# A recurrent attention block feeding a multiplicative FFN: the first group of the bridge tensor is carried on chip by thirty small DMAs, and three chunks' output stores change place in SyncE's queue

## The chip, the cores and the metric

The kernel runs on one core of one Trainium2 chip. The metric is the time of one execution on the device, in microseconds; lower is better. A profiled execution also has a span, the time from its first to its last instruction.

Five engines run side by side, each through its own list of instructions in order: TensorE (PE in the profile, its weight loads PEld), VectorE (DVE), ScalarE (ACT), GpSimd (POOL) and SyncE (SP). They wait for each other by semaphores. SP computes nothing here: it issues DMAs, which the core's 16 DMA engines carry out. SBUF is the on-chip memory of 128 partitions, PSUM the memory that TensorE writes to (eight banks here), DRAM the memory off the chip.

## What is computed

Two blocks follow each other. The first is a gated linear recurrence over 768 steps, for 4 batches and 8 heads of width 48; the second is a feed-forward block over the 3072 tokens that result, with 384 features:

```python
for t in range(S):
    state = alpha[:, :, t, :, None] * state + np.einsum('bhd,bhe->bhde', k[:, :, t], v[:, :, t])
    y[:, :, t] = np.einsum('bhd,bhde->bhe', q[:, :, t], state)
...
x = y.transpose(0, 2, 1, 3).reshape(B * S, H * D)     # 3072 x 384
a = x @ w1                                            # 384 x 1024
b = x @ w2
h = a * b @ w3                                        # 1024 x 1024
out = h @ w_out                                       # 1024 x 384
```

q, k, v and alpha are float32. The four weights are float64; the kernel reads them as pairs of 32-bit words ("raw") and converts them itself.

## The kernel before

**Chunks and groups.** The 3072 tokens are cut into 24 chunks of 128 tokens, six a batch. Three chunks make a group of 384 tokens; there are eight groups. In the first part of the program, `for n in range(N + 1)`, chunk n goes through the recurrence, and as soon as the first groups are complete the first layers of the feed-forward block (the "gates") are mixed in. The second part finishes the gates, folds w3 with w_out and projects.

**One chunk.** Its k and q arrive in a tile `kq` of 128 tokens x 2 x 8 heads x 48 (`load_kq`, lines 153 and 154: two DMAs of 192 KB in runs of 192 bytes), its alpha in a tile `ac` (line 147, 192 KB; chunks 2 to 7 in pairs, line 143). ScalarE takes the logarithm of alpha, TensorE sums it along the chunk (`decays`), ScalarE exponentiates. Then:

- `decayed`, line 359, on VectorE: `qk` = k and q times the decays. Iteration n does it for chunk n + 2.
- `transposed`, line 381, on TensorE: `qk` turned, for chunk n + 1 in iteration n; ScalarE copies it out of PSUM (line 383).
- `scores`, line 454, on TensorE, for chunk n; VectorE masks the scores into `ms` (line 457).
- `attend_state` (line 474) and `attend` (line 485), on TensorE, for chunk n - 1; ScalarE copies the result out of PSUM into the tile `x` (line 489): partitions 0 to 47 hold the even half of the heads' features, partitions 64 to 111 the other, so that a head has 48 partitions. `outer` (line 393) updates the state.

**Weights.** Beside this, raw pieces of w1 and w2 of 512 KB are loaded by SP (line 236, in `to_fp32`) and converted in steps by ScalarE and VectorE (lines 244 to 265; `convert` and `fetch` deal them out, `raws` says how many pieces may be under way). A third part of the split weight is made on TensorE (`third`, lines 276 and 277) and copied by ScalarE (line 278).

**The bridge.** `attend` appends two stores of the tile `x` to the list `later`: to `xd`, a tensor in DRAM for each group, in the layout features x tokens. `store()`, the first call of each iteration, issues them on SP (line 305: 96 KB each, 192 runs of 512 bytes). When a group is complete, `load_x` reads `xd` back into the tile `xT` of 128 partitions x 3 x 384 tokens (line 501, 576 KB); for group 0 that is done in iteration 4. `split_x` makes from `xT` the three parts of `x3` that the gates multiply with (line 507 on ScalarE, 508 and 509 on VectorE); for group 0 in iteration 6 = `FIRST`. The gates' matrix products are line 515. Every group's `xd` is read back again in the second part, for the other half of the gates.

**What sets the order.** Each engine runs its list in order. The list is not the order of the source: a scheduler of the tile framework sorts the instructions of each engine by its own estimate of when their inputs come, within the marks that the program sets (`after_marks`). SP's list holds all loads of q, k, v, alpha and raw weights and the stores together, in the order of their calls. The framework gives SP's DMAs eight completion semaphores in turn: in the built program each DMA on SP first waits until the DMA eight places ahead of it, which uses the same semaphore, has landed. The trace shows the same: eight semaphores in rotation, each DMA waiting for the one that it will update. So SP has at most eight DMAs under way.

The iteration's beginning, in the source:

```python
store()
if n in loads:
    load_x(loads[n])
if n != 1 and not 2 < n <= FIRST:
    load_a(n + 5)
...
for m in (n + 3,) * (n <= FIRST) + (n + 4,) * (n >= FIRST):
    load_kq(m)
    if 2 < n <= FIRST and m == n + 3:
        load_a(n + 5)
    if n < FIRST - 2:
        fetch(raws)
```

Of the kernel before, what the change touches and what calls it, by code (L numbers as in the profile page):

```python
# [10 lines left out]
FP32 = mybir.dt.float32  # L11
# [37 lines left out]
def kernel(  # L49
# [12 lines left out]
    nc = tc.nc  # L62
    B, H, S, D = q.shape
    C = 128
# [5 lines left out]
    DP = 64  # L70
    Q = 32
    KM = DM // C
# [3 lines left out]
    TG = G * C  # L76
# [8 lines left out]
    def pool(name, bufs, stack=ctx, **kw):  # L85
        return stack.enter_context(tc.tile_pool(name=name, bufs=bufs, **kw))
# [3 lines left out]
    xp = pool("xp", 1)  # L90
# [18 lines left out]
    st, mark = {}, {}  # L109

    def after_marks(*names):
        stack = ExitStack()
        for x in names:
            stack.enter_context(tc.issue_after(mark[x]))
        return stack
# [5 lines left out]
    xd = [dram.tile([DM, TG], FP32, name=f"xd{g}") for g in range(NG)]  # L121
# [9 lines left out]
    def rows(src, n):  # L131
        b, c = divmod(n, NCH)
        return src[b, :, ds(c * C, C), :].rearrange("h p d -> p h d")

    def paired(n):
        return 2 <= n < PAIRED

    def load_a(n):
        if paired(n):
            if n % 2 == 0:  # L140
                b, c = divmod(n, NCH)
                x = pairs[n // 2 % 2]
                nc.sync.dma_start(out=x.rearrange("p h s d -> p h (s d)"), in_=alpha[b, :, ds(c * C, 2 * C), :].rearrange("h (p s) d -> p h (s d)", s=2))
                st["a", n] = st["a", n + 1] = x
        elif n < N:
            st["a", n] = inp.tile([C, H, D], FP32, tag="ac", name="ac", bufs=2)
            nc.sync.dma_start(out=st["a", n], in_=rows(alpha, n))

    def load_kq(n):
        if n >= N:  # L150
            return
        st["kq", n] = inp.tile([C, 2, H, D], FP32, tag="kq", name="kq")
        nc.sync.dma_start(out=st["kq", n][:, 0], in_=rows(k, n))
        nc.sync.dma_start(out=st["kq", n][:, 1], in_=rows(q, n))

    def load_v(n):
        if n < N:
            st["v", n] = vs[n % len(vs)]
            (nc.gpsimd if 2 < n < 8 else nc.sync).dma_start(out=st["v", n][:, :, 0:D], in_=rows(v, n))

    def turned(n):
        return TURNED <= n < N
# [117 lines left out]
    def fetch(ahead=3):  # L280
        while weights and len(begun) < ahead:
            begun.append(weights.popleft())
            next(begun[-1])
# [15 lines left out]
    later = deque()  # L299

    def store():

        while later:
            dst, src = later.popleft()
            nc.sync.dma_start(out=dst, in_=src)
# [171 lines left out]
    def attend(n):  # L477
        (y, heads), ms, vc = st.pop(("y", n)), st.pop(("ms", n)), st.pop(("v", n))
        for j, i, to in heads:
            if turned(n):  # L480
                w = vts[n % 2][:, j, :] if i else vc[:, 2 * j, :]
                nc.tensor.matmul(to[:, DP:], w, ms[:, i, j, DP:], start=False,  # L482
                                 stop=(j % HP == HP - 1), skip_group_check=True)
            else:
                nc.tensor.matmul(to, vc[:, 2 * j + i, :], ms[:, i, j, :], start=(n % NCH == 0 and j % HP == 0),  # L485
                                 stop=(j % HP == HP - 1), skip_group_check=True)
        x = work.tile([C, HP, 2, C], FP32, tag="x", name="x", bufs=4)
        for i in range(2):
            copied = nc.scalar.copy(x[:, :, i], y[i])
        ends_of_part1[1] = copied.ins  # L490
        x = x.rearrange("p j i t -> p (j i) t")

        g, c = divmod(n, G)
        to = xd[g].rearrange("(b h d) t -> b d h t", b=2, d=D)
        for half in range(2):
            later.append((to[half, :, :, ds(c * C, C)], x[ds(DP * half, D)]))


    def load_x(g, queue=nc.sync):
        st["xT", g] = xp.tile([C, KM, TG], FP32, tag="xT", name="xT")  # L500
        queue.dma_start(out=st["xT", g], in_=xd[g].rearrange("(k p) t -> p k t", p=C))

    def split_x(g, i):
        x = st.pop(("xT", g))
        t = tr[i].tile([C, 3 * KM * TG], FP32R, tag="x3", name="x3").rearrange("p (s k t) -> p s k t", s=3, k=KM)
        st["x3", g] = t
        nc.scalar.activation(t[:, 0], x, AF.Copy, scale=1.0 - 2.0 ** -13)
        nc.vector.tensor_sub(t[:, 1], x, t[:, 0].bitcast(FP32))
        mark["x3"] = nc.vector.scalar_tensor_tensor(t[:, 2], t[:, 0].bitcast(FP32), -1.0 - 1.0 / P, x,  # L509
                                                    op0=ALU.mult, op1=ALU.add).ins  # L510
# [73 lines left out]
    def gate(g, f):  # L584
        yield from (late_gate if late else early_gate)(g, f)
# [99 lines left out]
    FIRST = 6  # L685
# [1 line left out]
    loads = {8: 1, 11: 2, 15: 3, 19: 4}  # L687

    for n in range(N + 1):
        store()  # L690
        if n in loads:
            load_x(loads[n])
        if n != 1 and not 2 < n <= FIRST:
            load_a(n + 5)
        raws = (3, 3, 3, 3, 2, 2, 3, 3)[n] if n < 8 else 4
        for m in (n + 3,) * (n <= FIRST) + (n + 4,) * (n >= FIRST):
            load_kq(m)
            if 2 < n <= FIRST and m == n + 3:
                load_a(n + 5)
            if n < FIRST - 2:  # L700
                fetch(raws)
        if n >= FIRST:
            load_v(n + 2)
        if n:
            attend_state(n - 1)
        if n < N:
            scores(n)
        else:
            for j in range(NP):
                for i in range(2):  # L710
                    attend_low(n - 1, j % 2, i, i ^ (j < 2))
        transposed(n + 1)
        if n == 1:
            decays(3)
            load_a(6)
            with after_marks(("e", 3)):
                logs(4)
        if n == FIRST + 1:
            run(2)
        if n < FIRST:  # L720
            with after_marks("pool"):
                load_v(n + 2)
        if n - 2 in begin and n > FIRST:
            g, tiles = begin[n - 2]
            with after_marks(("ms", n), ("qkT", n + 1)):
                split_x(g, 0)
            fill.extend(gate(g, f) for f in tiles)
        if n == FIRST:
            with after_marks("l", ("qkT", n + 1)):
                split_x(0, 0)  # L730
            fill.extend(gate(0, f) for f in begin[n - 3][1])
        pieces = ((3, 3, 2, 0) if n > FIRST + 3 else (0, 3, 3, 0))[(n - FIRST) % 4] if n >= FIRST else 0
        if n == 0:
            with after_marks(("qkT", 0)):
                logs(2)
            decays(2)
            with after_marks(("e", 2)):
                logs(3)
        early, ready = n < FIRST, len(thirds) if n > 2 else n // 2
        marks = (*[("qkT", n + 1)] * (n < N - 1), *[("qk", n + 1), ("ms", n)] * early, *["x3"] * (n - 2 in begin and n > FIRST))  # L740
        if n < N - 2 and n != FIRST:
            with after_marks(*marks):
                convert(2 if early else 1, raws)
        advance(n)
        turn_v(n)
        if n:
            attend(n - 1)
        outer(n)
        if n > FIRST:
            third(ready)  # L750
        run(pieces > 0)
        if early:
            with after_marks(*marks):
                convert(1, raws)
        with after_marks(*[("ms", n)] * (n < 3)):
            decayed(n + 2)
        if not early:
            with after_marks(*[("qkT", n + 1)] * (n < N - 4)):
                logs(n + 4)
        if n == 4:  # L760
            load_x(0)
        convert(early and n > 0, raws)
        run(pieces > 1)
        if n:
            decays(n + 3)
        if n <= FIRST:
            third(ready)
        if 0 < n < FIRST:
            with after_marks(("e", n + 3)):
                logs(n + 4)  # L770
        if n == FIRST:
            with after_marks("x3", ("e", n + 3)):
                convert(2, raws)
        elif n < N - 2:
            convert(n == FIRST - 1 if early else n % 3 == 0, raws)
        if n == FIRST - 1:
            assert len(done) == 2 * KM
        run(pieces > 2)
        if n == N - 3:
            while begun:  # L780
                convert(1)
            weights.extend(load_out(j) for j in range(KF))
            fetch(4)
# [90 lines left out]
```

## Time and profile before

| what | value |
|---|---|
| runs | 466.03 us median of 3 (464.22 to 467.32) |
| the profiled execution's own time | 465.8 us |
| its span | 464.1 us |
| PE busy | 446.0 us (96%) |
| DVE busy | 371.1 us (80%) |
| ACT busy | 276.3 us (60%) |
| DMA packets | 148869, 80.37 MB, mean 173 GB/s |
| loads of k and of q | 24 each of 192 KB |
| stores of x to `xd` | 48 of 96 KB, 4.0 us from issue to landing (median) |
| read-back of `xd` on SP | 5 of 576 KB, 4.7 us |

The busy times are those of the whole span. The page also cuts the span into 40 slices of 11.6 us, with a digit for the busy tenths of each engine, the granted TensorE clock and the DMA engines. A "chain" view follows the program back from its last instruction, at each step to what released it. A "timeline" lists instructions with their start, their length and, in brackets, the idle time before them and what ended it. A tile's view gives the DMAs that touch it and the time from issue to landing. A busy PE is not PE at its peak, since matrix products are pipelined.

### The profile page before, as it was taken

What the parts mean: (1) busy time and instruction counts of PE and PEld (TensorE: products, weight loads), DVE (VectorE), ACT (ScalarE), POOL (GpSimd) and SP (SyncE); (2) the same over time, 40 slices, a digit from 0 to 9 for tenths busy, and PEclk for the clock granted to TensorE, in tenths of its full rate; (3) what the DMA queues carried; (4) which work ended last, traced back from release to release, by engine and by line L of the source; (5) the groups of instructions that cost most, each with busy time, mean ns of one, the idle gap of its engine ahead of it and who ended that gap; (6) DMA issues with size and microseconds to landing.
All of it is one profiled execution on the core that took longest, in us unless ns stands there. A gap on an engine that the chain in (4) does not pass through costs nothing.

```text
span 464.1 us, 11153 instructions
## 1 busy us (share of the span) xinstructions
PE 446.0 (96%) x4296; PEld 424.3 (91%) x4296; DVE 371.1 (80%) x610; ACT 276.3 (60%) x544; POOL 94.3 (20%) x186
## 2 busy tenths in 40 slices
PE   4996999899999999999999999999999999999996
PEld 2674899799999989999999999999999999999996
DVE  2886997999979989899998999997542967776671
ACT  4764984848668553989875776764544543333430
POOL 6332152215322360112221201211110000000000
PEclk9998899999999999999999999999999999999999
DMA  9999999899998965476766446412115966655511
GB/s 174 257 208 235 245 221 206 203 216 230 173 223 178 239 185 154 126 227 211 216 187 204 131 142 177 148 52 86 51 37 153 260 200 180 186 176 162 164 51 52
DMA packets 148869, 80.37 MB, mean 173 GB/s; under 512 B 97392, under 2 KB 138608, under 8 KB 148816
## 3 DMA queue, kind: packets, MB, share of 16 engines
q1 hardware_dynamic: 143040, 64.44, 57.2%
q0 software_dynamic: 5776, 15.22, 10.8%
q8 instruction: 34, 0.56, 0.6%
q14 instruction: 19, 0.16, 0.1%
HBM read 57.58 MB, written 22.06 MB: 172 GB/s over the span
## 4 chain that ended last, share of the span: by engine, by line
PE 87%; DVE 5%; DMA 4%; issue 2%; ACT 1%; SPq 0%; DVEq 0%
PE bank L515 71%; DMA kq<-in_q_dram 4%; PE bank L381 3%; PE bank L430 2%; PE bank L474 2%; PE bank L482 2%; PE bank L454 1%; PE bank L393 1%; PE bank L343 1%; PE bank L346 1%; PE bank L485 1%; PE bank L419 1%; DVE ms L457 1%; DMA ac<-in_alpha_dram 1%; DVE x L509 1%
## 5 line engine op out<-in xcount | busy, mean ns | idle before, releaser
L515 PE MATMUL bank<-x,w 128*128 128x384 f32 x1152 | 209.5, 337 | 1.0 <-DVE ms L440 0.9
L515 PEld LDWEIGHTS bank<-x,w 128*128 128x128 f32 x1152 | 200.2, 188 | 2.8 <-DVE ms L440 1.2
L515 PE MATMUL bank<-w3o,ab 128*128 128x384 f32 x576 | 100.2, 336 | 0.0
L515 PEld LDWEIGHTS bank<-w3o,ab 128*128 128x128 f32 x576 | 99.9, 188 | 0.0
L540 ACT ACTIVATE bank<-bank 128x384 f32<-128x384 f32 x96 | 45.7, 476 | 43.5 <-PE bank L515 43.2
L524 ACT ACTIVATE t<-bank 128x384 f32<-128x384 f32 x64 | 31.6, 495 | 55.1 <-PE bank L515 54.8
L590 POOL DMA_DIRECT2D abd<-ab x45 | 25.8, 573 | 137.7 <-DVE ab L576 121.5
L383 ACT COPY qkT<-bank 128x512 f32<-128x512 f32 x48 | 26.0, 593 | 24.2 <-PE bank L381 24.2
L641 DVE TENSOR_TENSOR ab<-abl,ab 128x1024 fp32r<-128x1024 f32 x24 | 29.4, 1224 | 12.5 <-ACT ab L640 12.5
L640 ACT ACTIVATE ab<-abl 128x1024 fp32r<-128x1024 f32 x24 | 25.5, 1061 | 20.2 <-PE bank L515 18.4
L515 PE MATMUL bank<-wo,w3T 128*128 128x384 f32 x192 | 35.9, 334 | 0.0
L359 DVE TENSOR_TENSOR qk<-kq,e 128x768 f32<-128x768 f32 x24 | 23.2, 966 | 15.4 <-ACT e L350 7.6
L576 DVE TENSOR_TENSOR ab<-bank,r 128x384 f32<-128x384 f32 x44 | 24.2, 550 | 12.5 <-PE bank L515 6.3
L515 PEld LDWEIGHTS bank<-wo,w3T 128*128 128x128 f32 x192 | 33.5, 188 | 0.0
L249 ACT ACTIVATE power<-power,rebias 128x512 uint32<-128x512 uint32 (+1 forms) x36 | 25.1, 698 | 11.2 <-DVE power L248 11.2
L526 DVE SCALAR_TENSOR_TENSOR o<-bank,t 128x384 f32<-128x384 f32 x24 | 13.4, 557 | 22.7 <-issue 13.7
L642 DVE SCALAR_TENSOR_TENSOR ab<-ab,abl 128x1024 fp32r<-128x1024 f32 x24 | 29.2, 1218 | 0.0
L526 DVE SCALAR_TENSOR_TENSOR r<-bank,t 128x384 f32<-128x384 f32 x40 | 22.1, 553 | 6.8 <-ACT t L524 3.4
L251 DVE SCALAR_TENSOR_TENSOR mant<-mant,rest 128x512 f32<-128x512 uint32 (+1 forms) x36 | 23.8, 661 | 3.4 <-ACT rest L244 3.3
L252 DVE SCALAR_TENSOR_TENSOR power<-raw,power 128x512 uint32<-128x512 uint32 (+1 forms) x36 | 23.6, 655 | 2.4 <-ACT power L249 2.4
L253 DVE TENSOR_TENSOR mant<-mant,power 128x512 f32<-128x512 f32 (+1 forms) x36 | 23.6, 656 | 0.5
L244 ACT ACTIVATE rest<-raw 128x512 f32<-128x512 uint32 (+1 forms) x36 | 23.3, 649 | 0.0
(102 smaller groups left out, 675.4 us busy)
## 6 DMA issues: line engine op xcount, KB each, us to landing
abl<-abd SPq DMA_DIRECT2D x24, 512.0 KB, 4.6
abd<-ab POOLq DMA_DIRECT2D x45, 192.0 KB, 3.1
raw<-in_moe_w_dram SPq DMA_DIRECT2D x64, 128.0 KB, 3.4
raw<-in_moe_w_dram SPq DMA_DIRECT2D x12, 512.0 KB, 6.2
xT<-xd POOLq DMA_DIRECT2D x9, 576.0 KB, 4.6
kq<-in_k_dram SPq DMA_DIRECT2D x24, 192.0 KB, 4.9
kq<-in_q_dram SPq DMA_DIRECT2D x24, 192.0 KB, 5.4
xd<-x SPq DMA_DIRECT2D x48, 96.0 KB, 4.0
```

Source lines behind the costliest of these rows:

```text
L249: nc.scalar.activation(power, power, AF.Relu, scale=2.0 ** 23, bias=rebias)
L251: nc.vector.scalar_tensor_tensor(mant, top, 2.0 ** -20, rest, op0=ALU.mult, op1=ALU.add)
L383: mark["qkT", n] = nc.scalar.copy(qkT[:, :, :, ds(DP * half, DP)], tp[half]).ins
L515: nc.tensor.matmul(p, w[part][i], x[part][i], start=start and part == parts[0] and i == 0, stop=stop and part == parts[-1] and i == n - 1, ...
L524: nc.scalar.activation(t, p1, AF.Copy, scale=(1.0 + 1.0 / P) * scale)
L526: nc.vector.scalar_tensor_tensor(to, p2, scale, t, op0=ALU.mult, op1=ALU.add)
L540: nc.scalar.activation(p, p, AF.Copy, scale=1.0 + 1.0 / P)
L576: nc.vector.tensor_mul(ab, p, r[0])
L590: (nc.gpsimd if late else nc.sync).dma_start(out=abd[g][:, f, :], in_=ab)
L640: nc.scalar.activation(t[:, 0], ab, AF.Copy, scale=1.0 - 2.0 ** -13)
L641: nc.vector.tensor_sub(t[:, 1], ab, t[:, 0].bitcast(FP32))
L642: nc.vector.scalar_tensor_tensor(t[:, 2], t[:, 0].bitcast(FP32), -1.0 - 1.0 / P, ab, op0=ALU.mult, op1=ALU.add)
```

## The change

The output of the first three chunks (group 0) no longer goes to `xd` and back before it is split. `attend` calls the new function `place`, which writes the tile `x` straight into the tile `xT`, from SBUF to SBUF: one DMA a head, and two where a head's 48 features lie across two blocks of 128 partitions. That makes ten DMAs a chunk, of 48, 32 or 16 partitions x 512 bytes (24, 16 or 8 KB), in place of two of 96 KB. `load_x(0)` in iteration 4 is gone. Since the second part still reads `xd[0]`, one store of the whole `xT`, 576 KB, is issued at the start of iteration 7 (`FIRST + 1`). And in iterations 2 to 5 the stores are issued after that iteration's loads of k, q and alpha and not ahead of them. `split_x` keeps `xT` in the table (no `pop`).

```diff
         g, c = divmod(n, G)
+        if g == 0:
+            return place(c, x)
         to = xd[g].rearrange("(b h d) t -> b d h t", b=2, d=D)
...
+    def place(c, x):
+
+        if ("xT", 0) not in st:
+            st["xT", 0] = xp.tile([C, KM, TG], FP32, tag="xT", name="xT")
+        for h in range(H):
+            half, j = divmod(h, H // 2)
+            f = h * D
+            while f < (h + 1) * D:
+                kk, at = divmod(f, C)
+                n = min(C - at, (h + 1) * D - f)
+                later.append((st["xT", 0][ds(at, n), kk, ds(c * C, C)], x[ds(DP * half + f - h * D, n), j]))
+                f += n
...
     def split_x(g, i):
-        x = st.pop(("xT", g))
+        x = st["xT", g]
...
     for n in range(N + 1):
-        store()
+        if not 1 < n < FIRST:
+            store()
         if n in loads:
             load_x(loads[n])
+        if n == FIRST + 1:
+            nc.sync.dma_start(out=xd[0].rearrange("(k p) t -> p k t", p=C), in_=st["xT", 0])
...
             load_kq(m)
             if 2 < n <= FIRST and m == n + 3:
                 load_a(n + 5)
+            if 1 < n < FIRST:
+                store()
             if n < FIRST - 2:
                 fetch(raws)
...
-        if n == 4:
-            load_x(0)
         convert(early and n > 0, raws)
```

**The built program.** TensorE's list is the same in both kernels. SP's has 14 rows more. The scheduler also sorts VectorE's and ScalarE's lists anew around the changed stretch:

```
VectorE, before: ms(3) w mant power qk(5) tmp .. qk(6) ms(4) w mant power T .. qk(7) ms(5) w mant power .. ms(6) w ms(6) qk(8) T x-split ..
VectorE, after:  qk(5) ms(3) w mant power tmp .. ms(4) w mant power qk(6) T .. ms(5) w mant power .. qk(7) w ms(6) T ms(7) x-split qk(8) ..
ScalarE, before: .. qkT(7) x-split x la e la e w w ..
ScalarE, after:  .. qkT(7) x e e w w x-split la ..
```

Numbers in brackets are chunks, and ".." leaves steps of a conversion out. On VectorE w, mant and power are steps of a weight's conversion; on ScalarE the "w w" are the copies of two thirds (line 278). x-split is the split of group 0 (lines 507 to 509 before, 521 to 523 after); tmp and T are updates of the state, ms(7) in the second line is its first half. Two passages carry most of the difference: qk(5) stands ahead of ms(3) and not qk(6) ahead of ms(4), and the split of group 0 stands ahead of qk(8) on VectorE and behind the copies of the thirds on ScalarE.

## The prediction

> **What bounds the kernel now.** The page first: busy shares, then the slices.
>
> ```profile
> PE 446.0 (96%) x4296; PEld 424.3 (91%) x4296; DVE 371.1 (80%) x610; ACT 276.3 (60%) x544; POOL 94.3 (20%) x186
> ...
> PE   4996999899999999999999999999999999999996
> ...
> PEclk9998899999999999999999999999999999999999
> DMA  9999999899998965476766446412115966655511
> ```
>
> From the fifth slice on (46 us), TensorE is full: the windows from 51 to 84 us and from 86 to 140 us show it busy all the time, with a gap of 1.5 us at 84. So a microsecond lost or won before the gates begin (line 515, first at 59.16 us) moves the end by as much, and the question is when TensorE gets there. The DMA engines are full just there too. The chain of the first 60 us says what TensorE waits for (start, length, what):
>
> ```profile
> 20.27 8.82 DMA kq<-in_q_dram
> ...
> 34.62 7.67 DMA kq<-in_q_dram
> 42.29 0.03 issue
> ...
> 42.84 0.25 DVE qk L359
> 43.09 0.62 issue
> 43.71 0.70 DVE ms L457
> 44.41 0.04 issue
> 44.45 0.80 PE bank L276
> ```
>
> The q of chunk 6 is issued at 34.62 and lands 7.67 us later. VectorE, which has qk(6) ahead of ms(4), is held until then, and TensorE with it: 3.59 us idle before 44.45 in its timeline. The windows show what follows (stretch, busy times of PE, PEld, DVE, ACT, POOL, then the clock, DMA share and GB/s):
>
> ```profile
> 44.00:51.00 7.00, 6.55 (x67) 5.28 (x68) 6.97 (x13) 4.21 (x9) 1.44 (x2) 0.56 1.00 228
> 51.00:59.00 8.00, 8.00 (x120) 6.36 (x122) 7.34 (x13) 7.72 (x18) 1.03 (x2) 1.00 1.09 229
> ```
>
> After the gap the clock is at half. The six groups from line 276 to line 485 take 44.45 to 50.84, 6.39 us; the same six take 51.29 to 55.26, 3.97 us, one pass later. So **a gap of that kind costs 2.4 us on top of itself**, and slows by a factor of 1.6. The change aims at this place: loads ahead of stores. SP's timeline shows what it moves (start, length, instruction):
>
> ```profile
> 28.01 1.91 SPq L305 DMA_DIRECT2D xd<-x  x2
> 30.02 0.39 SPq L153 DMA_DIRECT2D kq<-in_k_dram  x1
> ...
> 42.21 0.40 SPq L153 DMA_DIRECT2D kq<-in_k_dram  x1
> ...
> 45.94 0.37 SPq L501 DMA_DIRECT2D xT<-xd  x1
> ...
> 47.37 0.50 SPq L153 DMA_DIRECT2D kq<-in_k_dram  x1
> ```
>
> **What the moved loads gain.** k and q of chunk 5 no longer wait for a chunk's stores: those are issued at 28.01 and end at 29.92, and on the DMA engines they take from 31.71 (the raw piece ahead landing) to 32.66, 0.95 us. Chunks 6 and 7 have one chunk's stores fewer ahead of them, 0.95 us. Chunk 8 also loses the 576 KB read-back ahead of it (45.94 to 50.71; the DMA ahead landed at 48.15, so 2.56 us of service). On the engines, q(5) lands at about 35.40 - 0.95 - 0.9 (GpSimd's v, issued at 29.03, now comes behind) = 33.6. But qk(5) now stands ahead of ms(3): ms(3) begins at 33.6 + 0.1 + 0.87 = 34.5 and not at 32.26, its first half is out at 35.2, and TensorE's line 276, at 33.69 before, waits for it: 1.5 us lost. ms(4) in turn no longer waits for q(6). TensorE reached that place at 40.86; plus 1.5, less the 0.63 us it waited at 36.25, that is 41.7 and not 44.45: 2.7 us won. With the half clock gone, 2.4 more: **5.1 us ahead at 51 us**, and TensorE done with scores(6) at 53.74 - 5.1 = 48.6. This is all that the change can win.
>
> **What the small DMAs cost on SP.** A DMA on SP waits until the one eight places ahead has landed. Before, that rarely decided: six DMAs a chunk. Now a chunk has fourteen: ten pieces, raw, k, q, alpha. From 27 to 58 us the tile views give from issue to landing (shortest, median, longest) 4.0, 4.6, 5.5 for the stores of x, 4.4, 5.0, 8.0 for k and q, 4.4, 4.9, 7.5 for alpha, 6.1, 6.4, 6.8 for raw. No row has a piece of 24 KB, SBUF to SBUF; the nearest is the 96 KB store of the same tile, so I take its 4.6. Fourteen DMAs then need (10 x 4.6 + 2 x 5.0 + 4.9 + 6.4) / 8 = **8.4 us a chunk**. Before, the stores' starts 28.01, 33.17, 40.08, 46.40 and 52.88 give 6.2. The low bound is SP's own issue time: 14 x 0.43 (a store's median) = 6.0, under 6.2, no cost. The high bound has every piece at raw's 6.4: 11.2 us.
>
> At 8.4, k of chunks 5, 6, 7 and 8 is issued at 28.0, 36.4, 44.8 and 52.4 (the last without a raw piece, 0.8 less); before at 30.02, 34.13, 42.21 and 47.37. The raw piece ahead of k(7) goes out 0.9 earlier, at 43.9, and lands at 50.3; before at 38.17 and 44.56.
>
> The Trainium skill has a rule for this term: "DMA: Bandwidth & Descriptors", section "Anatomy of one DMA", gives about 2.0 us fixed plus bytes over 436 GB/s for a DMA issued by GpSimd. A piece would land after an estimated 2.06 us, before seven more are issued; SP would never wait, and the sum would be that of the low bound. [...] The stage's rows, at twice that and more, speak against it.
>
> **What that does to the engines.** VectorE now has the steps on this raw piece (lines 245 to 253) ahead of qk(7); before, qk(7) ran at 48.39 and these steps from 51.06 to 53.96, 2.9 us. So qk(7) is out at 50.3 + 0.1 + 2.9 + 0.95 = 54.2, and line 381 of chunk 7 follows at 54.25, before at 53.74. TensorE has been idle since 48.6: the 5.1 us won are lost here, 0.5 more, and the gap, longer than 3.59, brings the half clock.
>
> Then the split of group 0. Its input is no trouble: the last piece goes out just ahead of k(8), at 52, and lands at 56.6. But ScalarE now has the split behind the copies of the two thirds, and VectorE has qk(8) behind its part of the split. From line 381 of chunk 7 (53.74) to the end of the second third (57.58) TensorE took 3.84; at half clock 3.84 x 1.6 = 6.2. Then a copy 0.59, ScalarE's split 1.22, VectorE's two 1.26 + 1.35, qk(8) 0.96, and 0.3 for hops: 5.7. Line 381 of chunk 8 comes at 54.25 + 6.2 + 5.7 = 66.1; before at 58.57. **That is 7.5 us late.** TensorE ended scores(7) at about 62, so it idles 4 us again: half clock again, 2.4. (Before, line 507 ran at 55.85, under other work, and nothing of this chain was on the path.)
>
> For the clock the skill agrees with the row and adds a condition: "TensorE: Matmul & The Clock Gate", section "What's actually happening", has windows of about 3.4 us that run free, so a gap near that length may or may not halve the clock. If neither gap did, the estimate would be 4.8 us lower.
>
> **Hidden.** The store of 576 KB in iteration 7 delays what stands behind it by 2.56 us of service; TensorE, late by more than the queue, covers it, else it costs those 2.56. The 1.5 us gap at 84 stands behind the split of group 1 and stays. Later groups, GpSimd's list and the second part do the same work.
>
> **The sum.** 7.5 + 2.4 = 9.9 us late at the gates, and TensorE is full from there to the end. The profiled execution: 465.8 + 9.9 = 475.7; against the median of 466.03 about the same, and I say 475.5.
>
> **Rivals.**
>
> - *The places never bind* (pieces landing within 3.4 us, eight issues). At 6.2 us a chunk raw lands at 39.5 + 6.4 = 45.9, qk(7) is out at 49.9, line 381 of chunk 8 comes at 49.9 + 3.84 + 5.7 = 59.4, 0.9 late, with or without 2.4 for the half clock: 466.7 to 469.1. For it: the pieces touch no DRAM. Against it: they queue behind the same loads. 0.22.
> - *The places bind harder*: 11.2 us a chunk puts raw's landing at 55.9, line 381 of chunk 8 at 71.7, 13.1 late, plus 2.4: 481.3. For it: the loads' 5 to 8 us, which the pieces now stand behind. Against it: stores landed in 5.5 at most. 0.13.
> - *Faster*: the won 5.1 us stay won, 460.7. This takes q and raw of chunk 7 on time and a split off the path; it decides if TensorE's idle time ahead of line 381 of chunk 8 is nil. For it: split inputs land early. Against it: the lists as built put the split there, which gives back 5.7 + 3.84 - 4.83 = 4.7 whatever the DMAs do. 0.05.
> - *It does not do what it says*: pieces late for the split, which then waits for a landing. Over 61 us it would decide; 5 us hence. In the forecast's range or above; 0.05.
>
> The forecast itself has 0.55. A difference under 1% can't be told from none here. Slower by over 1% (from 470.7) are the forecast, the harder rival and the last one, less 0.01 that may fall short: 0.72. Same is the first rival and that 0.01: 0.23. Faster is 0.05. The range leaves out the faster end and most of the harder one: 467 to 480.5.
>
> **What would show it.** SP's DMAs near 8.4 us a chunk, with the DMA share under 1 between 34 and 56 us; qk(7) ending at 54, TensorE idle over 3.5 us ahead of line 381 of chunks 7 and 8, both with the half clock behind; line 521 beginning after 60 us. I am wrong if SP's chunk takes 6 to 7 us, if TensorE keeps its clock, or if later slack takes the delay back.

## The result, and the profile after

The changed kernel takes **480.19 us** (median of 4 runs, 479.67 to 480.80), the kernel before 465.75 (4 runs): a ratio of 1.0317, with a 95% interval of 1.0278 to 1.0355. It is slower, by 14.4 us. The prediction said 475.5, slower by 9.5, with 467 to 480.5 as its range: the sign was right, the loss was half as large again as forecast, and 480.19 lies at the very end of the range (1.0317 times the 466.03 us that the prediction started from is 480.8, just past it). The profiled execution took 479.67, with a span of 478.0; before, 465.8 and 464.1. So the spans differ by 13.9 us, and against the prediction's own sum of 9.9 there are 4.0 us to explain.

The page of the changed kernel, with the lines that answer to those shown of the kernel before:

```profile
PE 451.1 (94%) x4296; PEld 428.5 (90%) x4296; DVE 372.5 (78%) x610; ACT 278.2 (58%) x544; POOL 94.7 (20%) x186
...
PE   4989469999999999999999999999999999999996
...
PEclk9997778999999999999999999999999999999999
DMA  9997589999899996466576554532102985555511
```

PE's dip now spans the fifth and sixth slices (48 to 72 us), not the fourth alone; the clock is below full in the fourth to seventh, and the DMA engines, full there before, are at five to eight tenths in the fourth to sixth (36 to 72 us). So TensorE waits while the DMA engines have room. SP's timeline in that stretch (start, length, instruction):

```profile
37.76 0.53 SPq L236 DMA_DIRECT2D raw<-in_moe_w_dram  x1
38.39 1.26 SPq L153 DMA_DIRECT2D kq<-in_k_dram  x1
39.70 0.57 SPq L154 DMA_DIRECT2D kq<-in_q_dram  x1
40.32 2.49 SPq L147 DMA_DIRECT2D ac<-in_alpha_dram  x1
42.91 7.66 SPq L305 DMA_DIRECT2D xT<-x  x10
50.68 0.54 SPq L236 DMA_DIRECT2D raw<-in_moe_w_dram  x1
51.31 0.38 SPq L153 DMA_DIRECT2D kq<-in_k_dram  x1
```

From one raw piece to the next, 37.76 to 50.68, SP needs 12.9 us, with hardly a gap between its instructions. The prediction had 8.4. Ten pieces hold it for 7.66 us, so the raw piece ahead of k of chunk 7 goes out at 50.68, where 43.9 was forecast, and lands at 54.35. TensorE's timeline (start, length, instruction; in brackets the idle time before it and what ended it) shows the price:

```profile
58.46 1.12 PE L381 MATMUL bank<-ident,qk 64*128 64x64 f32 x16 [6.81 <-DVE qk L359]
...
64.83 1.16 PE L454 MATMUL bank<-qkT 48*128 48x128 f32 x16
70.49 0.94 PE L381 MATMUL bank<-ident,qk 64*128 64x64 f32 x16 [4.50 <-DVE qk L359]
71.36 4.69 PE L529 MATMUL bank<-x,w 128*128 128x384 f32 x18
```

These are line 381 of chunks 7 and 8, each behind a long idle time, and the first group of the gates, which at half clock takes 4.69 us (3.40 before). Line 381 of chunk 8 is 11.9 us later than before (58.57), the second group of gates 13.5 (77.46 against 63.97), the end 13.9.

### The profile page after: what moved, and what is told of

Same layout as the page of the kernel before. It is cut to its first block, busy times and chain, and to the rows that moved or that the text cites. A ratio compares the mean times of both kernels' runs of the same rounds, so it can differ in the third digit from the quotient of the medians.

```text
span 478.0 us, 11195 instructions
## 1 busy us (share of the span) xinstructions
PE 451.1 (94%) x4296; PEld 428.5 (90%) x4296; DVE 372.5 (78%) x610; ACT 278.2 (58%) x544; POOL 94.7 (20%) x186
## 3 DMA queue, kind: packets, MB, share of 16 engines
q0 software_dynamic: 5776, 15.22, 10.2%
## 4 chain that ended last, share of the span: by engine, by line
PE 83%; DMA 6%; DVE 4%; SPq 3%; ACT 2%; issue 2%; DVEq 0%; ACTq 0%
PE bank L529 70%; PE bank L430 3%; DMA kq<-in_q_dram 3%; SPq L305 3%; PE bank L381 2%; PE bank L482 2%; PE bank L474 2%; DMA ac<-in_alpha_dram 1%; PE bank L346 1%; PE bank L393 1%; DMA raw<-in_moe_w_dram 1%; PE bank L419 1%; DMA kq<-in_k_dram 1%; DMA raw<-in_moe_w_out_dram 1%; PE bank L343 1%
## 5 line engine op out<-in xcount | busy, mean ns | idle before, releaser
L381 PE MATMUL bank<-ident,qk 64*128 64x64 f32 x384 | 18.7, 241 | 14.8 <-DVE qk L359 13.8
L381 PEld LDWEIGHTS bank<-ident,qk 64*128 64x128 f32 x384 | 15.6, 150 | 18.1 <-ACT w L260 7.0
```

Of the source, the lines that this page charges most:

```text
L381: nc.tensor.transpose(tp[half][:, i, j, :], qk[s, i, 2 * j:2 * j + 2, :], ident[s, s])
```

## The experiments

The theory after reading both traces, **A**: SP is bound by the time it takes to issue a DMA, not by places or landings; thirty pieces at about 0.63 us each lengthen its chunk, and whatever stands behind them in its queue comes late. (SP issues 340 DMAs in the trace of the changed kernel and 316 in that of the kernel before: 24 more, thirty pieces and one store in place of six stores and a read-back, and not the 14 rows named above.) Rivals: **B**, the path from SBUF to SBUF or the new order costs; **C**, the prediction's places, eight at a time, wait for landings; **D**, the place of group 0's split has a price of its own. The ratios below are to the kernel before, measured on the same chip.

### Each part alone

Stores behind the loads, on the kernel before (`loads_first`):

```diff
-        store()
+        if not 1 < n < FIRST:
+            store()
...
                 load_a(n + 5)
+            if 1 < n < FIRST:
+                store()
             if n < FIRST - 2:
```

> One part of the change alone, on the kernel before: in iterations 2 to 5 the stores of x go out behind that iteration's loads; two stores of 96 KB a chunk to DRAM and the read-back of group 0 stay as they were. Theory A (the ten pieces a chunk are what costs; SP issues each in about 0.63 us): with two stores a chunk none of the 14 us appears; 461 to 467 us. Within A, if the 5.1 us that the prediction counts as won by the moved loads are real, 460.7; if the list with qk(5) ahead of ms(3) opens a pause near 34 us and so only moves the half clock there, as in the changed kernel (1.90 us idle before 35.70, clock 0.57 from 36 to 44), 464 or more. Theory B (the order of loads and stores, with the lists it brings, is what costs): 472 us or more.

Measured: 465.28 us, ratio 0.9997 (0.9982 to 1.0013). The reordering costs nothing, and it brings nothing either. The 5.1 us that the prediction counted as won are not there, though the half clock is gone. The window from 44 to 51 us (stretch; busy times of PE, PEld, DVE, ACT, POOL; clock, DMA share, GB/s):

```profile
44.00:51.00 7.00, 6.02 (x87) 4.35 (x88) 6.97 (x14) 4.97 (x11) 2.11 (x4) 1.00 1.20 211
```

At full clock TensorE now has a microsecond of small waits here, and VectorE is busy for 6.97 of 7 us. Line 454 of chunk 6 begins at 50.86 (52.74 before), 1.9 us earlier, the first gates at 58.27 (59.16), 0.9 earlier, and the span is 0.7 shorter. The pause ahead of line 276 that the expectation feared near 34 us was only 0.49 us long here, at 36 us, and the clock stayed up; so neither account of the missing gain in that expectation was right.

The ten pieces alone, with the stores ahead of the loads as before the change (`place_only`: the changed kernel with `store()` again the first call of each iteration):

> The other part alone, on the changed kernel: ten pieces a chunk on chip, but the stores go out first in every iteration, as before the change. Theory A (SP's issue time for thirty pieces): each chunk's ten pieces of 0.63 us now stand straight ahead of its k and q, SP's chunk stays at 10 to 13 us, and the time is that of the changed kernel or more: 478 to 486 us. Theory B (the loads' order costs): near the kernel before, 466 to 470.

Measured: 475.31 us, ratio 1.021 (1.0171 to 1.0248). SP's chunk is 9.5 and 10.2 us, from the starts of its ten pieces at 26.17, 35.64 and 45.86, and line 381 of chunk 7 begins at 58.59, as late as in the changed kernel. But the time is below what was expected. The last ten pieces stand ahead of k of chunk 7 in this order and not ahead of k of chunk 8, which goes out at 56.66 (61.18 in the changed kernel); line 381 of chunk 8 begins at 65.58 after 0.20 us of idle time. So of the 14.4 us some 10 come with the pieces wherever they stand, and the stores' new place, harmless by itself, adds 4 to 5 to them.

In this run, unlike in the changed kernel, the prediction's limit of eight did hold SP. Four pieces (at 30.20, 31.67, 40.38 and 41.60) go out 0.02 us after the DMA eight places ahead has landed, and the view of SP's waits from 24 to 62 us (line, what it waited for: us, times, longest) has 2.2 us of them, a little over one microsecond in each of the two chunks:

```profile
SPq L305 <- DMA raw<-in_moe_w_dram: 1.3, 2, 0.9
...
SPq L305 <- DMA xT<-x: 0.7, 1, 0.7
...
SPq L305 <- DMA x<-in_alpha_dram: 0.2, 1, 0.2
```

### The number of pieces, their size, their way

Two pieces in place of ten, same place, SBUF to SBUF (`two_pieces`):

```diff
-        for h in range(H):
...
+        for half in range(2):
+            later.append((st["xT", 0][ds(DP * half, D), :, ds(c * C, C)], x[ds(DP * half, D), 0:KM]))
```

> The changed kernel with two DMAs a chunk in place of ten, same place in SP's queue, same tiles: 48 partitions x 3 x 512 bytes each, 72 KB. The heads land in the wrong rows of the tile and one head in four is left out, so the feed-forward of group 0 computes on other data; the tile is zeroed once on GpSimd. All else does the same work. Theory A (issue time): SP is spared 8 x 0.63 = 5 us a chunk, raw ahead of k of chunk 7 goes out 7 to 10 us earlier than 50.68, and the time falls to 461 to 468 us. Theory B (what costs is the path itself, SBUF to SBUF with late landings, or the split's place): 474 us or more.

Measured: 466.62 us, ratio 1.003 (1.0009 to 1.0051). The path from tile to tile by itself is not what costs. Nor does it gain: with nearly the whole loss gone, the kernel is still no faster than with a store to DRAM and a read-back.

Ten pieces of a quarter of the length (`small_pieces`):

```diff
-  st["xT", 0][ds(at, n), kk, ds(c * C, C)],      x[ds(DP * half + f - h * D, n), j]
+  st["xT", 0][ds(at, n), kk, ds(c * C, C // 4)], x[ds(DP * half + f - h * D, n), j, 0:C // 4]
```

> The changed kernel with the ten pieces a chunk kept, but each a quarter as long (32 tokens, 128 bytes a partition, 2 to 6 KB); three quarters of group 0's input are left out and stay zero. The lists of all engines are those of the changed kernel. Theory A (SP's issue time, whatever the size): SP's chunk stays at 12 to 13 us and the time within 1.5 us of 480.2. Theory C (the prediction's: the places bind, so the landing counts, or the bytes): pieces that land sooner shorten the chunk, 475 us or less.

Measured: 480.81 us, ratio 1.0344 (1.0284 to 1.0403). A quarter of the bytes changes nothing; from one raw piece to the next SP still needs 12.1 us (37.85 to 49.98).

Five pieces a chunk (`five_pieces`: only those with `half == 0`):

> The changed kernel with only the first five of the ten pieces a chunk (the even half of the heads); the other half of group 0's input is left out and stays zero. The lists of VectorE and ScalarE come out a little different from the changed kernel's (the split of group 0 is earlier). With two pieces a chunk the time was 466.62, with ten 480.19. If each piece costs its issue time, whatever else is late (linear): 466.62 + 15 x 0.57 = 475, so 472 to 477 us. If there is a threshold (SP's chunk of four loads and five pieces, 5 x 0.63 + 2.0 to 4.9 = 5 to 8 us, is not longer than the 6.0 to 7.5 us that the engines take for a chunk, so that the pieces are hidden until SP's chunk exceeds that): 466 to 470 us.

Measured: 472.27 us, ratio 1.0148 (1.0110 to 1.0187). Two, five and ten pieces a chunk give 466.62, 472.27 and 480.19: 0.63 us for each of the first nine DMAs added and 0.53 for each of the next fifteen (0.60 and 0.49, when each is first taken against the kernel before on its own chip). That is close to the time that SP takes to issue one, 0.63 with its gap. At neither of these two steps do the added pieces hide.

Ten pieces, but to DRAM, with the read-back as before (`ten_stores`: the reordered kernel above, its two stores of the first three chunks cut at the change's borders):

```diff
+        if g == 0:
...
+                    n = min(C - f % C, (h + 1) * D - f)
+                    later.append((xd[0][ds(f, n), ds(c * C, C)], x[ds(DP * half + f - h * D, n), j]))
```

> The count without the path: x of the first three chunks goes to DRAM and is read back in iteration 4, as before the change, with the stores behind the loads, but each chunk's stores are cut into the change's ten pieces (48, 32 or 16 partitions x 512 bytes) in place of two of 96 KB; nothing is left out. Theory A (the number of DMAs on SP is what costs, wherever they go): with two stores of the same bytes this order took 465.28; with ten, SP's chunk is 10 to 13 us again and the time is 474 us or more, near 480 if a piece to DRAM takes 0.6 us to issue, near 474 if it takes the 0.43 of a 96 KB store. Rival (the way from SBUF to SBUF costs): within 2 us of 465.3.

Measured: 474.51 us, ratio 1.0202 (1.0136 to 1.0267). The same bytes on the same way take some 9 us more as ten DMAs than as two. And a piece to DRAM is issued faster than one to SBUF. The tile views of the changed kernel and of this run (length on SP, shortest, median and longest, in ns; then issue to landing):

```profile
L305 SPq DMA_DIRECT2D xT<-x x30: 536/589/2678, 29.3 to 60.1; - x30
...
DMA to landing us min/median/max: 1.7/2.5/5.5
```

```profile
L305 SPq DMA_DIRECT2D xd<-x x32: 368/420/2474, 28.9 to 61.1; - x32
...
DMA to landing us min/median/max: 1.5/2.3/5.6
```

0.59 us against 0.42 (the 32 hold two stores of chunk 3). Thirty differences of 0.17 make 5.1 us, and the two kernels lie 5.7 apart (5.3, each against the kernel before on its own chip). That the first makes the second is argued from the sizes: the two kernels also differ in the read-back.

### What stands behind the pieces

The raw weights ahead of the pieces (`raw_first`: `store()` moved behind the iteration's first `convert`, which issues them):

> The changed kernel with one swap in SP's queue: in iterations 2 and 3 the 512 KB piece of raw weights that stood behind the ten pieces of x goes out ahead of them; the lists of VectorE and ScalarE up to the gates stay. In the changed kernel SP issued ten pieces from 44.02 to 50.57, then raw at 50.68, k and q of chunk 7 at 51.31 and 51.74, which landed at 54.35, 55.40 and 56.45; line 381 of chunk 7 began at 58.46. Theory A1 (the issue time of the pieces is the loss, and q of chunk 7 is as late as raw): raw is early, but q still waits for the pieces; it lands 1 to 2 us earlier at most, line 381 of chunk 7 begins at 56 to 57.5, and the time is 477 to 479.5 us. Theory A2 (the ring raw, ScalarE's lines 244 and 249, x copy, ten pieces, next raw is the loss, and breaking it gives most of it back): 473 us or less.

Measured: 477.04 us, ratio 1.0226 (1.0172 to 1.0279), as A1 has it. The raw piece is off the path now, and qk of chunk 7 waits for q: SP issues the ten pieces from 43.27 to 50.34 and then k and q; qk begins at 54.57 (57.36 in the changed kernel), line 381 at 55.68, a little ahead of what was expected. (In the changed kernel the ten pieces begin at 42.91; 44.02 is the second one.) Whatever comes first, something that is needed is behind 7 us of pieces.

The pieces on another queue (`pool_pieces`):

```diff
-            nc.sync.dma_start(out=dst, in_=src)
+            (nc.gpsimd if len(dst.shape) == 2 else nc.sync).dma_start(out=dst, in_=src)
```

> The changed kernel with the thirty pieces issued by GpSimd in place of SP; nothing is left out. SP's chunk then has four DMAs, and its raw piece ahead of k of chunk 7 goes out before 44. Theory A (SP's issue time): the 14 us are gone unless GpSimd has no room for them: 462 to 468 us. GpSimd's DMAs took 0.5 to 0.9 us each to issue in the changed kernel, so ten pieces are 5 to 9 us a chunk there, ahead of its update of the state (line 412) that TensorE's line 474 waits for; if that decides (rival), line 474 is late in each of three chunks and the time is 470 or more.

Measured: 477.95 us, ratio 1.0251 (1.0208 to 1.0295). The rival holds: SP is free, and GpSimd is not. It needs 0.50 us a piece, and its own work stands behind them, the loads of v and the update of the state. Its pieces also wait for earlier DMAs of its own queue to land, six times and 3.9 us in all; they land after 4.7 us in the median. The view of GpSimd's waits from 24 to 62 us, and TensorE's timeline:

```profile
POOL xT L305 <- DMA xT<-x: 3.0, 4, 1.2
...
POOL xT L305 <- DMA v<-in_v_dram: 0.9, 2, 0.5
```

```profile
45.75 1.09 PE L393 MATMUL bank<-v,qk 128*64 128x48 f32 x16 [5.17 <-DMA v<-in_v_dram]
56.81 1.13 PE L474 MATMUL bank<-qkT,T 48*64 48x128 f32 x16 [6.25 <-POOL T L412]
```

### The place of the split

The order of the kernel before at the split (`split_late`: `split_x(0, 0)` called behind `decayed(8)` and issued after `qk` of chunk 8, the copies of two thirds after ScalarE's part of it):

> The changed kernel with the order of the kernel before at one place: VectorE's qk of chunk 8 stands ahead of its part of the split of group 0, and ScalarE's part of the split ahead of the copies of two thirds. SP's list up to there stays. In the changed kernel line 381 of chunk 8 began at 70.49, 4.50 us after TensorE fell idle. Theory D (the split's place is a term of its own, as the prediction has it): qk of chunk 8 is ready at 66 to 68, line 381 of chunk 8 begins at 66.3 to 68.5, and the time falls by 2 to 4.9 us, to 475.3 to 478.2 (the upper end by the two masks that still stand ahead of qk; the lower by the run with the pieces ahead of the loads, whose list has qk ahead too and which took 475.3). Rival (SP's lateness alone sets the time, and the split's place is hidden behind q of chunk 8, landed at 65.25): within 1 us of 480.2.

Measured: 481.11 us, ratio 1.0327 (1.0272 to 1.0382): no gain. VectorE's two masks of chunk 7 still stood ahead of qk, which began at 68.19. So a further run puts qk ahead of these too (`qk_first`):

```diff
         for i in range(2):
+            with after_marks(*[("qk", n + 1)] * (n == FIRST + 1)):
-            masked = nc.vector.tensor_tensor(...)
+                masked = nc.vector.tensor_tensor(...)
```

> The run before it on this point put qk of chunk 8 ahead of the split, but the two masks of chunk 7, which wait for its scores, still stood ahead of qk: qk began at 68.19, as the second mask ended, and nothing was gained. Here VectorE has qk of chunk 8 ahead of both masks and of the split; all else as there. Theory D (the order on VectorE is a term of its own beside SP's lateness): qk of chunk 8 begins as q of chunk 8 lands, at 65 to 66.5, line 381 of chunk 8 at 66 to 67.5 and not at 70.49, TensorE is idle for less than 1 us there and keeps its clock, and the time is 474.5 to 477.5 us. Rival (SP's lateness alone sets the time; what is won here is lost again at the first gates, which wait for the split): 479 us or more.

Measured: 479.77 us, ratio 1.0305 (1.0261 to 1.0348). Where theory D looks, it is nearly right: qk of chunk 8 begins at 66.11 as q lands, line 381 at 67.22 after 1.60 us of idle time (under 1 was expected), and the second group of gates at 73.44, 4.0 us ahead of the changed kernel. But this does not reach the end: the time is the rival's, though the gain is lost later than at the first gates. The 28th copy of line 383 begins at 113.13 (116.69 in the changed kernel), the 31st at 127.22 (127.56): 3.2 of 3.6 us are lost in between. TensorE's timeline and the window there:

```profile
120.99 0.67 PE L393 MATMUL bank<-v,qk 128*64 128x48 f32 x16 [1.02 <-DMA v<-in_v_dram]
122.94 0.67 PE L475 MATMUL bank<-qkT,T 48*64 48x128 f32 x16 [0.74 <-DVE ms L440]
```

```profile
124.00:132.00 8.00, 8.00 (x115) 7.72 (x112) 7.80 (x13) 4.31 (x10) 3.02 (x4) 0.81 0.99 222
```

Two pauses, the first for a load of v, and again a stretch below full clock. The lists of VectorE, ScalarE and SP from the split on differ in this kernel, so whether a gain of this kind is always lost there, or by this list, stays open. No version run here beats the kernel before.

## Why the prediction was right in sign and wrong in what holds SP

**What bounds the kernel, and where a delay counts.** This part was right for delays: the gates' second group is 13.5 us late and the end 13.9. It was not wholly right for gains: the 4 us of the last run were lost again between 113 and 127 us. "TensorE is busy all the time" does not exclude that a load is just in time behind it.

**The step that failed** is "What the small DMAs cost on SP". It said that a DMA waits until the one eight places ahead has landed, and it put 8.4 us on a chunk, from landings divided by eight. The wait is in the program, and in the changed kernel it held nothing. In the trace the DMA eight places ahead of every one that SP issued between 27 and 62 us had landed at least 1.5 us earlier, never more than five others were under way, and the view of SP's waits in this stretch (line, what it waited for: us, times, longest) names only engines:

```profile
SPq L305 <- ACT x L316: 2.2, 1, 2.2
SPq L305 <- ACT power L249: 0.8, 1, 0.8
SPq L153 <- DVE power L252: 0.7, 1, 0.7
SPq L305 <- ACT x L489: 0.6, 2, 0.3
SPq L305 <- ACT w L260: 0.2, 1, 0.2
```

These five lie inside the length of an instruction, where the view goes by the last step that an engine reported. The waits for places in the run with the ten pieces alone show otherwise, as gaps of 0.2 to 1.0 us ahead of a start. Here the only pause between two of SP's DMAs longer than about 0.1 us is 0.5 us ahead of k at 61.18, so hardly any of SP's time in this stretch was a wait that the trace can show.

The limit can act: it did for 2.2 us where the ten pieces stood ahead of the loads, and landed after 4.2 us in the median. Here they landed after 2.5.

In its place stands SP's own time. From 37.76 to 50.68, by the starts: raw 0.63, k 1.31, q 0.62, alpha 2.59, the first piece 1.11 (not a wait for ScalarE's copy of x, line 489: by the order of copies and stores, the copy that these pieces carry had ended by 38.53), eight pieces 0.63 each, the last 1.65; 12.9 in all. The prediction had this term, as its *low* bound, "14 x 0.43 = 6.0, under 6.2, no cost". Two things were wrong with it. The 0.43 was a store's, and a piece to SBUF takes 0.59 and a gap of 0.05. And 0.43 was one row's median, while the timeline of the kernel before already showed q and alpha at 0.65 to 2.55 us on SP. In that kernel too SP's DMAs follow each other between 27 and 62 us with pauses of about 0.1 us at most, but for two of 0.5 and 0.9. (Its view of SP's waits has 10.8 us there, nearly all of it inside instructions; alpha loads with such an entry took 2.24 and 2.21 us, those without 2.55 and 2.11.) So a chunk's 6.2 us were already nearly full of SP's own lengths, and eight more DMAs at 0.63 make an estimated 11.2, not 6.0. Measured were 12.9 here, and 9.5 and 10.2 in the run with the ten pieces alone, a little over 1 us of each a wait for places. The loads' own lengths differ that much: alpha held SP for 2.49 us here and for 0.79 there. What holds SP in the long instructions was not told apart, so the 1.7 us above the estimate here, like the 2 to 3 below it there, stay open.

**How 9.9 became 13.9.** Raw was issued 6.8 us later than forecast but landed after 3.67 us and not 6.4, so 4.1 later in sum. That the forecast came this near is in part luck: two errors of opposite sign, 6.8 and 2.7 us, met in one term. The steps behind it held to 0.3 us: line 381 of chunk 7 at 58.46, that is 4.2 later than the forecast 54.25; from there to the end of the second third 6.44 us (forecast 6.2; 3.84 x 1.6 is 6.1), and from there to line 381 of chunk 8 5.59 (5.7). Line 381 of chunk 8 came at 70.49, forecast 66.1: 4.4 later. The half clock behind the second gap cost 1.6 and not 2.4 (13.5 less 11.9), and 0.4 was added later. 4.4 - 0.8 + 0.4 = 4.0.

**What the moved loads gain.** This was wrong by more, but cost the forecast little, since the pieces buried it. The reordering alone won 1.9 us at chunk 6 and not 5.1. In that run VectorE works from 41.79 to 56 us with no pause longer than 0.19, and two of TensorE's three waits between 43 and 51 us end with a step of VectorE's (lines 457 and 403); so VectorE, and not q of chunk 6 alone, set the pace. In the changed kernel line 454 of chunk 6 began at 50.49, 2.3 us earlier than before, and here the clock took a part: the pause ahead of line 276 that the prediction valued at 1.5 us was 1.90 us, and the clock halved behind it:

```profile
36.00:44.00 8.00, 8.00 (x85) 6.74 (x84) 6.68 (x13) 5.42 (x12) 2.02 (x5) 0.57 0.90 182
```

**The split's place.** It was counted at 5.7 us and took 5.6. Moving qk ahead of it won 3.3 at line 381 and 4.0 at the gates, though nothing of it was left at the end.

**The rivals.** "The places never bind" was true of the places in this kernel and wrong in its time, since it took the low bound for what was left. "The places bind harder" had nearly the right time (481.3), by a mechanism that did not act in this kernel; a quarter of the bytes leaves the time as it was. (Its chunk of 11.2 us takes all fourteen DMAs at 6.4; with the ten pieces alone at 6.4, as the prediction words it, the sum is 10.7.) The pieces were not late for the split: the last landed at 62.34, ScalarE's part of it began at 65.62.

**The rules weighed.** From "DMA: Bandwidth & Descriptors", section "Anatomy of one DMA", the Trainium skill's 2.0 us fixed gave the conclusion that SP never waits for a place. For the changed kernel that conclusion was right, and the stage's rows that were set against it were not the ones to take: the pieces landed after 2.5 us in the median, after 1.7 at the least, below the rule's fixed part. For the run with the ten pieces alone, where they landed after 4.2, the rows were nearer. On GpSimd's queue, the one of the rule, the median was 4.7. The same page says in "Rules for kernel authors" that many small transfers should be made into one large one, and in "Issuing engines are not separate DMA queues" that the time to initiate a DMA is usually small beside the DMA itself. The first was the rule for this change; it speaks of overhead under 64 KB, and pieces of 8 to 24 KB cost 0.53 to 0.63 us each here. The second does not hold for such pieces: 0.59 us on SP, a quarter of the 2.5 us to landing, is what decided.

## What to carry to other kernels

Count the DMAs that a change adds to a queue before its bytes: here each cost the kernel 0.5 to 0.6 us, and a quarter of the size cost the same, because the queue that issues them had less room in a pass than they take. To see that, lay the lengths of a queue's own instructions end to end over one pass and compare them with the pass; a limit on what is under way counts only if the trace shows an instruction that waited for it, as it did in some of the runs here and not in the changed kernel. And moving pieces to another queue moves what they delay: look first at what stands behind them there.

## What was not expected of the hardware

- A DMA of 8 to 24 KB takes SP 0.59 us to issue when it goes from SBUF to SBUF and 0.42 when the same piece goes to DRAM; GpSimd took 0.50. A quarter of the bytes left the 0.59 as it was (0.588).
- Where the DMA engines had room (a share of 0.44 from 44 to 51 us of the changed kernel), the soonest of such pieces landed after 1.7 to 1.8 us, less than half of the 4.0 to 5.5 us of the 96 KB stores before.
- A pause of 1.90 us ahead of line 276 was followed by a clock of 0.57 for 8 us, one of 1.99 in the run with small pieces by 0.58. One of 1.50 us at 84 us in the kernel before and one of 1.13 with five pieces left it at 1.00, but so did one of 2.33 us ahead of line 381 of chunk 8 in the run with ten stores, while 1.02 and 0.74 us close together in the last run were followed by 0.81. The prediction had only the 3.59 us of one row to go by. "TensorE: Matmul & The Clock Gate", section "What's actually happening", has windows of about 3.4 us that run free; these pauses, all shorter, show no single length that decides.
- The traces' own clock records agree with such windows. In all twelve kernels every stretch at half clock between 15 us and the last 30 us lasts 3.41, 6.83 or 10.24 us, and where a trace has several, they start a whole number of 3.41 us apart (in the changed kernel at 36.63, 53.70 and 70.77). So where a pause lies against these steps may count beside its length; no run here varied that alone.
